# Banded attention in front of a gated MLP: scores by strips of 32 queries with 64 keys in place of blocks of 64 with 96

## The chip, the cores and the metric

The kernel runs on one core of a Trainium2 chip. The metric is device time in microseconds of one execution; 0.5% is about 4.7 us. The engines are named as in the profile: PE is TensorE (its weight loads are listed apart as PEld), DVE is VectorE, ACT is ScalarE, POOL is GpSimd, and SP is the queue that issues most transfers.

## What is computed

Eight batches of eight heads, 576 positions, 64 wide. Half of the heads look back over 32 positions, the other half over 128 positions in steps of 4. The attention output of all heads is one row of 512 per position, and 4608 such rows go through a two-layer MLP with a gate.

```python
scores = scale * np.matmul(q, k.transpose(0, 1, 3, 2))
rel = pos[:, None] - pos[None, :]
mask_plain = (rel >= 0) & (rel < window)                                          # window = 32
mask_dil = (rel >= 0) & (rel < window * dilation) & (rel % dilation == 0)         # dilation = 4
...                                     # heads 0-3 plain, heads 4-7 dilated; softmax over keys
x = attn_out.transpose(0, 2, 1, 3).reshape(B * S, H * D)
h = x @ w_in                                                                      # 512 -> 2048
g = h * erf(softplus(h))
out = g @ w_out                                                                   # 2048 -> 512
```

## The kernel before

**Attention units.** The host puts the positions of a dilated head in order of their residue by 4, so that both kinds of head become the same thing: a query sees the 32 keys up to its own place (a mask cuts it where a residue begins). A block is 64 queries of two heads. Four blocks are a unit, and there are 72 units. In one unit:

- `scores` (lines 180 to 187) multiplies, for each block and head, 64 queries by the 96 keys that they can see: 8 matmuls with 64 rows, 64 columns and 96 streamed keys. The four positions (head by odd or even block) lie in four quarters of the 128 x 128 array. The results of head 0 go to PSUM bank sp0, those of head 1 to sp1.
- `mask_max` (189) adds a mask, and takes the maximum of every row, with four VectorE instructions over 128 rows (two blocks) and 96 keys; `exponents` (201) is four ScalarE instructions; `normalize` (212) takes the reciprocal of the sums on VectorE and multiplies on GpSimd, 4 x 96 columns.
- `transposes` (220) turns each of the four 128 x 96 groups on TensorE, so that keys lie on partitions; `turned` (225) copies the 96 x 512 result from PSUM to the tile pT.
- `values` (234) multiplies, for each block and head, the 64 columns of values by 64 turned queries, over 128 rows of which 32 are zero: 8 matmuls with 128 rows, 64 columns and 64 streamed queries. The two heads lie in the two halves of the array's columns and write two halves of one PSUM bank.
- `rows_hi` on ScalarE and `rows_lo` on VectorE (278 and 282) write the result as a rounded part and the rest.

All of these are 32-bit matmuls, and each appears in the trace as two matmuls and two weight loads; a transpose appears as one of each.

**The MLP.** Rows go in 9 chunks of 512, and the 2048 inner columns in 8 pairs of tiles. For every tile `mm1` (450) issues 12 matmuls of 512 rows (line 460: high by high, high by low and low by high part, over four parts of the 512), VectorE copies h out of its one bank (`take`, 465), ScalarE and VectorE form the gate, and `mm2` (489) issues 12 matmuls (line 501) into the four banks acc two steps later. The weights come as 64-bit words, and ScalarE and VectorE split them into two parts in the first third of the program (`prep_act`, `prep_dve`, 377 and 391).

**Order.** It is written out by hand. In the front, 14 units are scored, one per call of `first_visit` (311): TensorE gets the transposes of unit n - 3, the scores of unit n, and then the values of unit n - 3. In calls 1 to 9 ScalarE makes the copy of `turned`, and then two steps of weight preparation, before it takes the values. After that a table (`visits`, 72) sets at which of the 144 steps of the MLP which units are scored. From the second step on, TensorE's order in such a step is `mm1`, the transposes of one or two units, `mm2`, their values, and then the scores of the units three further on (lines 589, 607, 620 and 631). PSUM is full: sp0, sp1, tx, h and the four acc.

Of the kernel before, what the change touches and what calls it, by code (L numbers as in the profile page):

```python
# [22 lines left out]
BLK = 64  # L23
NBLK = S // BLK
KEYS = BLK + WIN
RES = S // DIL
DM, DF = 512, 2048
NTOK = B * S
# [2 lines left out]
TOK = 512  # L31
NCH = NTOK // TOK
NIT = B * HP

PER = 4
NU = NIT * NBLK // PER
NEG = -1.0e9
SCALE = 0.125
BIG = 3.0e38


EDGES = (0, 16, 32, 48, -16)
DIL_EDGE = {0: 0, 2: 1, 4: 2, 6: 3, 7: 4}

REBASE = 2.0 ** -112
# [14 lines left out]
LAG = 3  # L62
FIRST = NBLK + LAG + 2

FREE = FIRST - LAG + 4
# [3 lines left out]
SAVED = 2 * (HALF + 1) + 1  # L69


def visits():
# [19 lines left out]

def kind(n):

    it, blk = divmod(n, NBLK)
    dil = it % HP >= HP // 2
    return 1 + DIL_EDGE[blk] if dil and blk in DIL_EDGE else (1 if blk == 0 else 0)

PAIRS = sorted({(kind(n), kind(n + 1)) for n in range(0, NIT * NBLK, 2)})
NMASK = len(PAIRS)


def key_start(u, j):

    return j * BLK + (WIN if (PER * u) // NBLK != (PER * u + j) // NBLK else 0)


QW = PER * BLK  # L110
KW = QW + 2 * WIN
# [3 lines left out]
def attn_moe_kernel(ctx: ExitStack, tc: tile.TileContext, qk, v, masks, eye, w_in, w_out, out):  # L115
    nc = tc.nc
# [5 lines left out]

    first = pool("first", 1)
    ident = first.tile([P, P], F32, name="ident")
    cst = first.tile([P, NMASK * KEYS], BF16, name="cst")
# [18 lines left out]
    vz = [one.tile([P, PER, 2, D], F32, name=f"v{i}") for i in range(2)]  # L144
    pz = [one.tile([P, PER, P], F32, name=f"pT{i}") for i in range(2)]

    spb = [ps.tile([P, TOK], F32, name=f"sp{i}") for i in range(2)]
    sps = [b[:, 0:PER * KEYS].rearrange("p (i b k) -> p i b k", i=2, k=KEYS) for b in spb]
# [4 lines left out]
    second = set()  # L153

    def place(u):

        return acc[(u + 1) % 4] if u < FREE else bank[:, PER * BLK:] if u in second else bank

    def turn_place(u):

        return place(u) if u < FREE else spb[u in second]


    xs = [one.tile([P, 2, S], F32R, name=f"x{cc}") for cc in range(CC)]
# [1 line left out]

    def load_qk(u):
        if u < NU:
            n = QW + key_start(u, PER - 1) + KEYS
            nc.sync.dma_start(out=qkz[u % 2][:, 0:n], in_=qk[u, :, 0:n])  # L170

    def load_v(u):
        if has(u):
            nc.sync.dma_start(out=vz[u % 2][0:KEYS], in_=v[u].rearrange("p (j h d) -> p j h d", j=PER, h=2))

    probs, maxes, sums, x_rows = {}, {}, {}, {}

# [1 line left out]

    def scores(u):  # L180
        i = u % 2
        for j in range(PER):
            at, r = QW + key_start(u, j), j % 2 * BLK
            for h in range(2):
                hs = slice(h * D, (h + 1) * D)
                nc.tensor.matmul(sps[h][r:r + BLK, i, j // 2, :], qkz[i][hs, j * BLK:(j + 1) * BLK],  # L186
                                 qkz[i][hs, at:at + KEYS], start=True, stop=True)

    def mask_max(u):
        pr = probs[u] = work.tile([P, PER, KEYS], F32, name="prob", bufs=LAG + 1)  # L190
        nmax = maxes[u] = small.tile([P, PER], F32, name="nmax", bufs=LAG + 1)
        for h in range(2):
            for p in range(PER // 2):
                n = PER * u + 2 * p
                nc.vector.tensor_tensor_reduce(  # L195
                    out=pr[:, 2 * h + p, :], in0=sps[h][:, u % 2, p, :], in1=mask[PAIRS.index((kind(n), kind(n + 1)))],
                    scale=-SCALE, scalar=BIG,
                    op0=ALU.add, op1=ALU.min, accum_out=nmax[:, 2 * h + p:2 * h + p + 1],
                )

    def exponents(u):
        nmax = maxes.pop(u)
        sums[u] = small.tile([P, PER], F32, name="ssum", bufs=LAG + 1)
        for j in range(PER):
            nc.scalar.activation(  # L205
                out=probs[u][:, j, :], in_=probs[u][:, j, :], func=AF.Exp,
                scale=-1.0, bias=nmax[:, j:j + 1], accum_out=sums[u][:, j:j + 1],
            )
        if u < FIRST:
            nc.gpsimd.tensor_scalar(sums[u], sums[u], 1.0e-9, None, op0=ALU.add)  # L210

    def normalize(u):
        rinv = small.tile([P, PER], F32, name="rinv")
# [4 lines left out]
        nc.gpsimd.tensor_tensor(probs[u], probs[u], rinv.broadcast_to([P, PER, KEYS]), op=ALU.mult)  # L218

    def transposes(u):  # L220
        pr = probs.pop(u)
        for j in range(PER):
            nc.tensor.transpose(out=turn_place(u)[0:KEYS, j * P:(j + 1) * P], in_=pr[:, j, :], identity=ident)  # L223

    def turned(u, copy):
        copy(out=pz[u in second][0:KEYS].rearrange("p j q -> p (j q)"), in_=turn_place(u)[0:KEYS])

    def turn(units):
        for u in units:
# [3 lines left out]

    def values(u):
        xp, vt, pt = place(u), vz[u % 2], pz[u in second]
        for j in range(PER):
            r = j % 2 * BLK
            for h in range(2):
                nc.tensor.matmul(xp[h * D:(h + 1) * D, j * BLK:(j + 1) * BLK], vt[:, j, h, :],  # L239
                                 pt[:, 2 * h + j // 2, r:r + BLK], start=True, stop=True)  # L240

    def attend(ready, scored):
        for u in ready:
# [64 lines left out]
    def has(u):  # L308
        return 0 <= u < NU

# [99 lines left out]
    h = ps.tile([P, TOK], F32, name="h")  # L410
# [3 lines left out]
    at = {0: [[x[:, i, 0:TOK] for x in xs] for i in range(2)]}  # L414
# [48 lines left out]
    hs, ls, gs = {}, {}, {}  # L463
# [49 lines left out]
    def save():  # L513

        o = doubles(2).bitcast(F32).rearrange("p n w -> p (n w)")
        spare = small.tile([P, DM], F32, name="o", bufs=1)
        for tt in range(TOK // P):
            part = [o[:, 0:DM], o[:, DM:2 * DM], spare, pz[1].rearrange("p j q -> p (j q)")][tt]
# [23 lines left out]

    with tc.manual_schedule():
        load_qk(0)
        nc.sync.dma_start(out=cst, in_=masks)
        for t in vz:
            nc.gpsimd.memset(t[KEYS:P], 0.0)
        nc.gpsimd.memset(pz[0][KEYS:P], 0.0)
        load_qk(1)
        nc.sync.dma_start(out=ident, in_=eye)  # L550
        for n in range(FIRST):
# [20 lines left out]
        for x in range(2 * (NT + 2)):  # L572
            t, j = divmod(x, 2)
# [66 lines left out]
                normalize(u)  # L640
            for m in ready:
                rows_lo(m)
            if x == SAVED + 2:
                nc.gpsimd.memset(pz[1][KEYS:P], 0.0)
        assert not todo and not prep and not staged and not begun and not made and not rest


# [24 lines left out]
def _keys(a):  # L672

    p = _padded(a).transpose(0, 1, 2, 4, 3).reshape(NIT, P, S + WIN)
    k = np.zeros((NU, P, KW), a.dtype)
    for n in range(NIT * NBLK):
        u, j = divmod(n, PER)
        it, blk = divmod(n, NBLK)
        k[u, :, key_start(u, j):key_start(u, j) + KEYS] = p[it, :, blk * BLK:blk * BLK + KEYS]
    return k  # L680


def _values(a):

    p = _padded(a)
    w = np.stack([p[..., i * BLK:i * BLK + KEYS, :] for i in range(NBLK)], axis=2)
    w = w.reshape(NU, PER, 2, KEYS, D).transpose(0, 3, 1, 2, 4)
    return np.ascontiguousarray(w).reshape(NU, KEYS, PER * 2 * D)


def _masks():
    import ml_dtypes

    i = np.arange(BLK)[:, None]
# [4 lines left out]
    m = np.concatenate([np.concatenate([masks[x] for x in pair]) for pair in PAIRS], axis=1)  # L699
    return np.where(m, 0.0, NEG / SCALE).astype(ml_dtypes.bfloat16)  # L700


# [27 lines left out]
```

## Time and profile before

| what | before |
|---|---|
| median of 3 runs | 941.26 us (939.98 to 943.89) |
| the profiled execution | 939.52 us, its span 937.7 us |
| TensorE busy, share of the span | 910.9 us, 97% |
| VectorE, ScalarE, GpSimd busy | 592.1, 642.2, 92.2 us |
| scores, line 186 (PE busy) | 38.36 us |
| transposes, line 223 | 42.78 us |
| values, line 239 | 46.88 us |
| mean granted clock of TensorE | 0.988 (0.87 from 0 to 78 us, 1.00 from there to 740 us) |

Busy time counts a matmul from its start to its modelled end, and many overlap, so the time that a group takes on TensorE is read from the distances between starts. A row of a line's view gives the count, minimum, median and maximum in ns, and the first and the last start. A row of the timeline gives a start, the time that the merged group covers, and its count. "128*64" behind MATMUL is the active rows and columns of the array.

### The profile page before, as it was taken

How to read it: one execution, taken by the hardware profiler on the slowest of the kernel's cores; microseconds unless marked ns; L12 is line 12 of the kernel's file. 1: busy time of each engine (PE TensorE's matmuls, PEld its weight loads, DVE VectorE, ACT ScalarE, POOL GpSimd, SP SyncE). 2: the span in 40 equal slices, each digit the busy share in tenths (PEclk: the TensorE clock that was granted, in tenths of full speed). 3: DMA queues.
4: the chain of work that ended last, by engine and by line, in shares of the span. 5: the costliest groups of instructions: out<-in, count | busy, mean ns of one | idle time of the engine just before them, and what ended most of it. 6: DMA issues, size and time to landing. Idle time of an engine off the chain costs nothing.

```text
span 937.7 us, 15922 instructions
## 1 busy us (share of the span) xinstructions
PE 910.9 (97%) x6048; PEld 744.3 (79%) x6048; DVE 592.1 (63%) x1569; ACT 642.2 (68%) x1202; POOL 92.2 (10%) x96
## 2 busy tenths in 40 slices
PE   4889999999999999999999999999999999999998
PEld 3567877888888888888888888888888888888886
DVE  6889989886566655565666566566665444345434
ACT  7889888885866866666678675966566555445553
POOL 2311210000111111011111110111111000000000
PEclk9699999999999999999999999999999999999999
DMA  8775443432632142324232162224210302011001
GB/s 285 258 253 180 154 156 136 157 113 105 185 111 67 67 158 70 108 68 126 73 112 82 52 224 78 100 70 130 84 70 34 115 20 71 1 46 45 1 1 45
DMA packets 51501, 98.74 MB, mean 105 GB/s; under 512 B 7136, under 2 KB 20192, under 8 KB 51424
## 3 DMA queue, kind: packets, MB, share of 16 engines
q1 hardware_dynamic: 51136, 97.19, 30.8%
q8 instruction: 48, 0.79, 0.3%
q10 hardware_dynamic: 288, 0.52, 0.1%
q14 instruction: 29, 0.24, 0.1%
HBM read 69.52 MB, written 27.26 MB: 103 GB/s over the span
## 4 chain that ended last, share of the span: by engine, by line
PE 89%; DVE 5%; ACT 2%; DMA 2%; issue 1%; SPq 0%; POOL 0%; POOLq 0%; DVEq 0%
PE h L460 41%; PE acc L501 40%; PE tx L239 3%; PE sp L186 3%; PE sp L223 3%; DVE w L402 1%; DMA qk<-in_qk_dram 1%; DVE w L403 1%; DVE prob L195 1%; DVE win_lo L397 1%; DMA dbl<-in_w_in_dram 0%; PE acc L223 0%; DVE w L401 0%; DVE s L483 0%; PE acc L239 0%
## 5 line engine op out<-in xcount | busy, mean ns | idle before, releaser
L468 DVE COPY hc<-h 128x512 f32<-128x512 f32 x144 | 99.4, 690 | 269.9 <-PE h L460 269.4
L460 PE MATMUL h<-x,win_hi 128*128 128x512 f32 x832 | 258.6, 392 | 1.9 <-DVE hc L468 1.8
L501 PE MATMUL acc<-wout_hi,ghi 128*128 128x512 f32 x576 | 227.5, 395 | 0.5 <-DVE dbl L519 0.3
L501 PE MATMUL acc<-wout_lo,ghi 128*128 128x512 f32 x576 | 224.5, 390 | 0.0
L472 ACT ACTIVATE s<-hc 128x1024 f32<-128x1024 f32 x72 | 76.4, 1061 | 193.3 <-DVE hc L468 193.1
L460 PEld LDWEIGHTS h<-x,win_hi 128*128 128x128 f32 x832 | 154.7, 188 | 35.8 <-DVE hc L468 2.7
L460 PE MATMUL h<-x,win_lo 128*128 128x512 f32 x416 | 162.1, 390 | 0.0
L501 PE MATMUL acc<-wout_hi,glo 128*128 128x512 f32 x576 | 158.8, 389 | 0.0
L218 POOL TENSOR_TENSOR prob<-prob,rinv 128x384 f32<-128x384 f32 x72 | 85.8, 1202 | 578.2 <-DVE ssum L216 281.2
L501 PEld LDWEIGHTS acc<-wout_hi,ghi 128*128 128x128 f32 x576 | 108.2, 188 | 22.9 <-DVE dbl L519 0.7
L501 PEld LDWEIGHTS acc<-wout_hi,glo 128*128 128x128 f32 x576 | 108.1, 188 | 22.6
L501 PEld LDWEIGHTS acc<-wout_lo,ghi 128*128 128x128 f32 x576 | 108.3, 188 | 21.6 <-DVE wout_lo L397 0.2
L205 ACT ACTIVATE prob<-prob,nmax 128x96 f32<-128x96 f32 x288 | 104.0, 364 | 3.1 <-DVE nmax L195 2.7
L487 DVE TENSOR_TENSOR glo<-s,ghi 128x512 fp32r<-128x512 f32 x144 | 100.2, 696 | 5.2
L483 DVE TENSOR_TENSOR s<-hc,s 128x1024 f32<-128x1024 f32 x72 | 96.9, 1346 | 5.6 <-ACT s L476 5.6
L473 ACT ACT_TABLE_LOAD x72 | 92.4, 1283 | 1.3
L476 ACT ACT_TABLE_LOAD x72 | 92.4, 1283 | 1.3
L460 PEld LDWEIGHTS h<-x,win_lo 128*128 128x128 f32 x416 | 78.1, 188 | 16.7
L195 DVE CUSTOM_DVE_ANT_0 prob<-sp,cst 128x96 f32<-128x96 f32 x288 | 54.7, 252 | 42.9 <-PE sp L186 42.8
L460 PE MATMUL h<-dbl,win_hi 128*128 128x512 f32 x256 | 80.7, 396 | 0.0
L486 DVE CAST ghi<-s 128x512 fp32r<-128x512 f32 x144 | 75.5, 525 | 2.5
L476 ACT ACTIVATE s<-s 128x1024 f32<-128x1024 f32 x72 | 76.4, 1061 | 0.8
(60 smaller groups left out, 897.0 us busy)
## 6 DMA issues: line engine op xcount, KB each, us to landing
xT<-rows SPq DMA_DIRECT2D x26, 576.0 KB, 4.8
v<-in_v_dram SPq DMA_DIRECT2D x72, 192.0 KB, 4.2
qk<-in_qk_dram SPq DMA_DIRECT2D x48, 272.0 KB, 3.9
dbl<-in_w_in_dram SPq DMA_DIRECT2D x16, 512.0 KB, 4.2
dbl<-in_w_out_dram SPq DMA_DIRECT2D x16, 512.0 KB, 3.3
qk<-in_qk_dram SPq DMA_DIRECT2D x24, 288.0 KB, 4.2
out_dram<-w SPq DMA_DIRECT2D x26, 256.0 KB, 2.2
x<-xT SPq DMA_DIRECT2D x8, 320.0 KB, 5.3
```

Source lines behind the costliest of these rows:

```text
L195: nc.vector.tensor_tensor_reduce(out=pr[:, 2 * h + p, :], in0=sps[h][:, u % 2, p, :], in1=mask[PAIRS.index((kind(n), kind(n + 1)))], scale ...
L205: nc.scalar.activation(out=probs[u][:, j, :], in_=probs[u][:, j, :], func=AF.Exp, scale=-1.0, bias=nmax[:, j:j + 1], accum_out=sums[u][:, ...
L218: nc.gpsimd.tensor_tensor(probs[u], probs[u], rinv.broadcast_to([P, PER, KEYS]), op=ALU.mult)
L460: nc.tensor.matmul(h, w[:, cc, ft * P:(ft + 1) * P], x[cc], start=(k == 0 and i == 0), stop=(k == CC - 1 and i == 2))
L468: nc.vector.tensor_copy(out=hs[t][:, j], in_=h)
L472: nc.scalar.activation(out=ls[t], in_=hs[t], func=AF.Sigmoid, scale=-1.0)
L473: nc.scalar.activation(out=ls[t], in_=ls[t], func=AF.Ln, bias=TINY)
L476: nc.scalar.activation(out=ls[t], in_=ls[t], func=AF.Erf, scale=-1.0)
L483: nc.vector.tensor_tensor(out=e, in0=hc, in1=e, op=ALU.mult)
L486: nc.vector.tensor_copy(out=ghi, in_=e[:, j])
L487: nc.vector.tensor_tensor(out=glo, in0=e[:, j], in1=ghi.bitcast(F32), op=ALU.subtract)
L501: nc.tensor.matmul(acc[tt], g[:, tt * P:(tt + 1) * P], w[:, ft, :], start=(first and w is wout_hi and g is ghi), stop=(last and g is glo))
```

## The change

A strip of 32 queries takes the place of the block of 64, and sees 64 keys. A unit is still 4 x 64 queries of two heads, now as 8 strips.

- The scores of a unit are 16 matmuls with 64 rows, 32 columns and 64 streamed keys; the eight positions (head by strip modulo 4) lie in eight pieces of the array, and four strips fill the 128 rows of a result.
- Masks, maxima, exponents and products go over four groups of 128 x 64, in place of 128 x 96. There are 10 mask tables as before.
- Two such groups, the two heads of four strips, lie side by side and are turned in one transpose of 128 x 128: 2 per unit in place of 4. The keys of head 0 come to partitions 0 to 63, those of head 1 to 64 to 127. The copy out of PSUM is 128 x 256 in place of 96 x 512, and its source is the upper half of a bank.
- The values of a unit are 16 matmuls with 64 rows, 64 columns and 32 streamed queries, head 0 in the corner of the array at row 0 and column 0, head 1 in the corner at 64 and 64. Both corners write one PSUM bank, in different partitions.
- The values tile is 128 partitions by 512 (256 KB per unit in place of 192), without rows of zeros, so the memsets go.

```diff
 def scores(u):
     i = u % 2
-    for j in range(PER):
-        at, r = QW + key_start(u, j), j % 2 * BLK
+    for s in range(SPU):
+        at, (p, r) = QW + key_start(u, s), divmod(s, SIDE)
         for h in range(2):
             hs = slice(h * D, (h + 1) * D)
-            nc.tensor.matmul(sps[h][r:r + BLK, i, j // 2, :], qkz[i][hs, j * BLK:(j + 1) * BLK],
-                             qkz[i][hs, at:at + KEYS], start=True, stop=True)
+            nc.tensor.matmul(sps[h][r * STRIP:(r + 1) * STRIP, i, p, :], qkz[i][hs, s * STRIP:(s + 1) * STRIP],
+                             qkz[i][hs, at:at + KEYS], start=True, stop=True,
+                             tile_position=(h * D, r * STRIP))
...
 def transposes(u):
     pr = probs.pop(u)
-    for j in range(PER):
-        nc.tensor.transpose(out=turn_place(u)[0:KEYS, j * P:(j + 1) * P], in_=pr[:, j, :], identity=ident)
+    for p in range(PARTS):
+        nc.tensor.transpose(out=turn_place(u)[:, p * P:(p + 1) * P],
+                            in_=pr[:, 2 * p:2 * p + 2, :].rearrange("p h k -> p (h k)"), identity=ident)

 def turned(u, copy):
-    copy(out=pz[u in second][0:KEYS].rearrange("p j q -> p (j q)"), in_=turn_place(u)[0:KEYS])
+    copy(out=pz[u in second][:, 0:PARTS * P], in_=turn_place(u))
...
 def values(u):
     xp, vt, pt = place(u), vz[u % 2], pz[u in second]
-    for j in range(PER):
-        r = j % 2 * BLK
+    for s in range(SPU):
+        qs = slice(s * STRIP, (s + 1) * STRIP)
         for h in range(2):
-            nc.tensor.matmul(xp[h * D:(h + 1) * D, j * BLK:(j + 1) * BLK], vt[:, j, h, :],
-                             pt[:, 2 * h + j // 2, r:r + BLK], start=True, stop=True)
+            hs = slice(h * D, (h + 1) * D)
+            nc.tensor.matmul(xp[hs, qs], vt[hs, s, :], pt[hs, qs], start=True, stop=True,
+                             tile_position=(h * D, h * D))
```

Here STRIP is 32, SIDE 4 (strips that fill 128 rows), SPU 8 (strips of a unit) and PARTS 2; KEYS is 64 in place of 96.

TensorE's rows at the transposes of one unit in the MLP's steps, before (sp_90 is bank sp0, x_100 the last part of x, acc_93 an accumulator):

```order
L460 MATMUL h<-x_100,win_hi 128x512 x2
L460 MATMUL h<-x_100,win_lo 128x512
L223 MATMUL sp_90<-ident,prob 96x128 x4
L501 MATMUL acc_93<-wout_hi,ghi 128x512
L501 MATMUL acc_93<-wout_lo,ghi 128x512
```

Four transposes of 96 turned keys stand there. TensorE's rows at the same place now, with the changed kernel's line numbers:

```order
L478 MATMUL h<-x_100,win_hi 128x512 x2
L478 MATMUL h<-x_100,win_lo 128x512
L239 MATMUL sp_90<-ident,prob 128x128 x2
L519 MATMUL acc_93<-wout_hi,ghi 128x512
L519 MATMUL acc_93<-wout_lo,ghi 128x512
```

The transposes stand at the same place, two in place of four. Behind `mm2` stand the values of that unit and the first scores of the next (pT_88 and v_87 are the turned probabilities and the values, sp_90 and sp_91 the two score banks), before:

```order
L501 MATMUL acc_95<-wout_hi,glo 128x512
L501 MATMUL acc_96<-wout_hi,glo 128x512
L239 MATMUL tx<-pT_88,v_87 64x64 x8
L186 MATMUL sp_90<-qk_84 64x96
L186 MATMUL sp_91<-qk_84 64x96
```

Eight value matmuls stand ahead of the scores. The same place now, on TensorE:

```order
L519 MATMUL acc_95<-wout_hi,glo 128x512
L519 MATMUL acc_96<-wout_hi,glo 128x512
L257 MATMUL tx<-pT_88,v_87 64x32 x16
L200 MATMUL sp_90<-qk_84 32x64
L200 MATMUL sp_91<-qk_84 32x64
```

Nothing changes its place among the stages. The values are 16 matmuls of 64 x 32 in place of 8 of 64 x 64, and the pair of scores (head 0, head 1) stands eight times in place of four.

More of the change, by code (lines that the diff above doesn't have):

```diff
@@ L24 @@
 NBLK = S // BLK
-KEYS = BLK + WIN
+STRIP = 32
+NSTRIP = S // STRIP
+KEYS = STRIP + WIN
 RES = S // DIL
@@ L93, in kind, with kinds, key_start @@
 def kind(n):
[L95 to L107, printed above, removed]
+    it, strip = divmod(n, NSTRIP)
+    at = strip * STRIP
+    if it % HP >= HP // 2:
+        e = (at + STRIP - 1) // RES * RES - at
+        return 1 + EDGES.index(e) if e > -WIN else 0
+    return 1 if strip == 0 else 0
+def kinds(u, p):
+    n = SPU * u + SIDE * p
+    return tuple(kind(n + i) for i in range(SIDE))
+PARTS = SPU // SIDE
+QUADS = sorted({kinds(u, p) for u in range(NU) for p in range(PARTS)})
+NMASK = len(QUADS)
+def key_start(u, s):
+    return s * STRIP + (WIN if (SPU * u) // NSTRIP != (SPU * u + s) // NSTRIP else 0)
 QW = PER * BLK
@@ L159, in turn_place @@
     def turn_place(u):
-        return place(u) if u < FREE else spb[u in second]
+        return (place(u) if u < FREE else spb[u in second])[:, PARTS * P:2 * PARTS * P]
     xs = [one.tile([P, 2, S], F32R, name=f"x{cc}") for cc in range(CC)]
@@ L202, in exponents @@
         nmax = maxes.pop(u)
-        sums[u] = small.tile([P, PER], F32, name="ssum", bufs=LAG + 1)
-        for j in range(PER):
+        sums[u] = small.tile([P, 2 * PARTS], F32, name="ssum", bufs=LAG + 1)
+        for j in range(2 * PARTS):
             nc.scalar.activation(
@@ L544, in attn_moe_kernel @@
         load_qk(0)
[L545 to L548, printed above, removed]
+        nc.sync.dma_start(out=cst[:, 0:NMASK * KEYS], in_=masks)
         load_qk(1)
@@ L675, in _keys @@
     k = np.zeros((NU, P, KW), a.dtype)
[L676 to L679, printed above, removed]
+    for n in range(NIT * NSTRIP):
+        u, s = divmod(n, SPU)
+        it, strip = divmod(n, NSTRIP)
+        k[u, :, key_start(u, s):key_start(u, s) + KEYS] = p[it, :, strip * STRIP:strip * STRIP + KEYS]
     return k
@@ L685, in _values @@
     p = _padded(a)
[L686 to L688 removed]
+    w = np.stack([p[..., i * STRIP:i * STRIP + KEYS, :] for i in range(NSTRIP)], axis=2)
+    w = w.reshape(NU, SPU, 2, KEYS, D).transpose(0, 2, 3, 1, 4)
+    return np.ascontiguousarray(w).reshape(NU, 2 * KEYS, SPU * D)
 def _masks():
     import ml_dtypes
[L694 removed]
+    i = np.arange(STRIP)[:, None]
     kk = np.arange(KEYS)[None, :]
@@ L698, in _masks @@
     masks = [ok] + [ok & ~((i >= e) & (kk < WIN + e)) for e in EDGES]
-    m = np.concatenate([np.concatenate([masks[x] for x in pair]) for pair in PAIRS], axis=1)
+    m = np.concatenate([np.concatenate([masks[x] for x in quad]) for quad in QUADS], axis=1)
     return np.where(m, 0.0, NEG / SCALE).astype(ml_dtypes.bfloat16)
```

40 lines of the change are left out of this document (19 added, 21 removed).

## The prediction

> **What bounds the kernel now.** I read the page first: which engine is busy and what ended last.
>
> ```profile
> span 937.7 us, 15922 instructions
> PE 910.9 (97%) x6048; PEld 744.3 (79%) x6048; DVE 592.1 (63%) x1569; ACT 642.2 (68%) x1202; POOL 92.2 (10%) x96
> PE 89%; DVE 5%; ACT 2%; DMA 2%; issue 1%; SPq 0%; POOL 0%; POOLq 0%; DVEq 0%
> ```
>
> TensorE holds the chain for 89% of the span. The average hides where it does not, so the second view is busy time by stretch (columns PE, PEld, DVE, ACT, POOL, then clock, DMA share, GB/s).
>
> ```profile
> 0.00:78.00 78.00, 56.31 (x685) 41.92 (x689) 63.42 (x257) 63.38 (x215) 19.75 (x37) 0.87 0.78 266
> 78.00:740.00 662.00, 660.71 (x4516) 542.60 (x4515) 441.21 (x1181) 477.36 (x898) 72.43 (x59) 1.00 0.32 106
> 740.00:937.70 197.70, 193.85 (x854) 159.77 (x852) 87.46 (x132) 101.48 (x92) 0.00 (x0) 1.00 0.12 40
> ```
>
> From 78 to 740 us TensorE is idle for 1.3 us out of 662. There the price of the change is TensorE's own time, and nothing that VectorE, ScalarE or GpSimd save counts. Before 78 us TensorE is idle for 22 us and other engines decide. After 740 us there is no attention work left. The same view for the three attention lines alone (first scores, then transposes, then values) counts what lies in the middle stretch.
>
> ```profile
> 78.00:740.00 662.00, 24.61 (x864) 18.94 (x862) 1.00 0.32 106
> 78.00:740.00 662.00, 29.54 (x224) 25.22 (x224) 1.00 0.32 106
> 78.00:740.00 662.00, 32.91 (x896) 28.63 (x896) 1.00 0.32 106
> ```
>
> A 32-bit matmul shows as two rows (8 per unit in the code, 16 in the trace) and a transpose as one (4). So 864/16 = 54 units are scored, 224/4 = 56 turned and 896/16 = 56 valued in it; the other 16 to 18 units lie before 78 us.
>
> Next, one visit with two units in TensorE's order of time (start, length of the merged group).
>
> ```profile
> 306.70 1.03 PE L223 MATMUL sp<-ident,prob 128*96 128x128 f32 x8
> 307.49 0.48 PE L501 MATMUL acc<-wout_hi,ghi 128*128 128x512 f32 x1
> ...
> 310.41 1.15 PE L239 MATMUL tx<-pT,v 128*64 128x64 f32 x32
> 311.50 0.89 PE L186 MATMUL sp<-qk 64*64 64x96 f32 x32
> 312.32 0.73 PE L460 MATMUL h<-dbl,win_hi 128*128 128x512 f32 x2
> ```
>
> To get a rhythm from merged groups I cut inside them, clear of the first one, and take the length less the last one's own duration: that is the time from first start to last start.
>
> ```profile
> 306.70 0.93 PE L223 MATMUL sp<-ident,prob 128*96 128x128 f32 x7
> ```
> ```profile
> 310.58 0.99 PE L239 MATMUL tx<-pT,v 128*64 128x64 f32 x28
> ```
> ```profile
> 311.64 0.74 PE L186 MATMUL sp<-qk 64*64 64x96 f32 x26
> ```
> ```profile
> 311.49 0.15 PEld L186 LDWEIGHTS sp<-qk 64*64 64x64 f32 x4
> ```
> ```profile
> 311.49 0.20 PEld L186 LDWEIGHTS sp<-qk 64*64 64x64 f32 x6
> ```
> ```profile
> 312.31 0.30 PEld L460 LDWEIGHTS h<-dbl,win_hi 128*128 128x128 f32 x2
> ```
>
> The durations of single ones are in the views of the lines (minimum/median/maximum in ns) and in the groups.
>
> ```profile
> L223 PE MATMUL sp<-ident,prob x228: 270/272/314, 74.0 to 733.7; 128*96 128x128 f32 x114
> ```
> ```profile
> L239 PE MATMUL tx<-pT,v x912: 222/222/271, 77.2 to 737.2; 128*64 128x64 f32 x183
> ```
> ```profile
> L186 PEld LDWEIGHTS sp<-qk x1152: 129/133/228, 3.5 to 695.4; 64*64 64x64 f32 x192
> L186 PE MATMUL sp<-qk x1152: 242/243/420, 3.5 to 695.5; 64*64 64x96 f32 x192
> ```
> ```profile
> L460 PEld LDWEIGHTS h<-x,win_hi 128*128 128x128 f32 x832 | 154.7, 188 | 35.8 <-DVE hc L468 2.7
> ```
>
> Transposes: 0.93 - 0.273 = 0.657 us for 6 steps, 109 ns each. Values run in pairs, one per half of the columns: 28 matmuls are 14 pairs, 0.99 - 0.222 = 0.768 us for 13 steps, 58 to 59 ns a pair. Scores run in fours, one per quarter of the array: 26 matmuls span six steps, 0.74 - 0.243 = 0.497 us, 82 ns a four. Loads: four start at once, the fifth begins only after 311.54, and the sixth starts at 311.49 + 0.20 - 0.133 = 311.56, so a load of 64 columns keeps its quarter for about 55 ns. Two loads of 128 columns are 0.30 - 0.188 = 0.112 us apart. That is 0.85 to 0.9 ns per column loaded.
>
> Streaming: 96 columns take 82 ns and 128 take 109, 0.84 ns per column and next to nothing fixed. 64 columns would take 55 to 56 by that. The values' 58 lies just above, and equals a load of 64 columns (55) and a short handover: load and stream are balanced there now. That balance is what the change touches.
>
> **The change part by part, per unit, in the middle stretch.**
>
> Transposes: 4 at 109 ns (436) become 2 with 128 columns loaded and 128 streamed, 112 ns by the 128-column loads: 224. Saved 0.212 us x 56 = -11.9 us.
>
> Values: 8 matmuls (16 rows) become 16 (32 rows) with half the rows and half the stream, and still 64 columns of weights each. Two corners of the array work at once, as two column halves do now: 16 rounds in place of 8. The stream falls to 32 x 0.84 = 27 ns, the load stays at 55 ns and the handover with it; the scores' row shows 55 with 64 rows, so halving the rows does not shorten it. 16 x 58 = 0.934 against 0.467: +0.467 us x 56 = +26.2 us. This is the term that decides. Its lower end is 16 x 55 (-3 us); if the load did not bind at all, see the first rival.
>
> Scores: 8 matmuls of 96 keys become 16 of 64 keys, on eight pieces of the array in place of four. A round streams 64 columns, 56 ns; its load of 32 columns, 28 ns, is hidden. The bounds: all eight at once, 4 rounds, 0.224 against 0.330 us, -0.106 x 54 = -5.7 us; or still only four at once, 8 rounds, 0.448, +0.118 x 54 = +6.4 us. The nearest row is the load view: four loads started within 0.15 - 0.13 = 0.02 us, 7 ns apart, so eight need about 50 ns, inside a round of 56. I take -5.7.
>
> The number of turns between array layouts in a visit (full, values, scores, full) stays. So the drains stay: 311.50 less the last values' start leaves some 0.15 us there, in both kernels.
>
> Sum of the middle: -11.9 + 26.2 - 5.7 = +8.6 us. VectorE's copy of 256 columns in place of 512, the smaller masks, exponents and products, all lie beside a full TensorE here and are worth nothing. The values load grows from 192 to 256 KB; the DMA share is 0.32 in this stretch, so it stays covered; if it did not, the price would be the 0.25 us a unit that 64 KB take at the front's 266 GB/s.
>
> The front, 0 to 78 us, has other rules.
>
> ```profile
> 13.00:37.00 24.00, 18.42 (x256) 13.63 (x252) 23.33 (x99) 22.46 (x84) 7.13 (x13) 0.68 0.85 284
> ```
> ```profile
> 21.70:42.10 20.40, 16.57 (x212) 12.32 (x209) 19.15 (x86) 17.02 (x72) 5.71 (x12) 0.50 0.83 283
> ```
> ```profile
> 30.32 0.62 ACT L383 CAST win_hi<-w 128x512 fp32r<-128x512 f32 x1
> ...
> 30.48 1.12 PE L239 MATMUL acc<-pT,v 128*64 128x64 f32 x16 [0.56 <-ACT pT L226]
> ...
> 30.84 0.68 ACT L388 ACTIVATE w<-dbl 128x512 f32<-128x512 f32 x1
> ```
> ```profile
> 44.76 0.83 POOL L218 TENSOR_TENSOR prob<-prob,rinv 128x384 f32<-128x384 f32 x1
> ```
> ```profile
> L468 DVE COPY hc<-h 128x512 f32<-128x512 f32 x144 | 99.4, 690 | 269.9 <-PE h L460 269.4
> ...
> L226 DVE COPY pT<-sp 96x512 f32<-96x512 f32 x57 | 36.6, 678 | 0.1
> ...
> L285 DVE TENSOR_TENSOR rows<-tx,rows 128x256 fp32r<-128x256 f32 x18 | 7.3, 419 | 0.0
> ...
> L226 ACT COPY pT<-acc 96x512 f32<-96x512 f32 x7 | 4.0, 572 | 0.4 <-PE acc L223 0.4
> ...
> L280 ACT CAST rows<-acc 128x256 fp32r<-128x256 f32 x3 | 1.1, 372 | 3.3 <-DVE nmax L195 1.7 <-PE acc L239 1.6
> ```
>
> From 13 to 37 us VectorE is full, 23.3 of 24. It pays (690 - 419)/256 = 1.06 ns per column, so four masks of 64 in place of 96 save 4 x 34 = 0.14 us a visit. But from 21.7 to 42.1 us the granted clock is 0.50, and every TensorE price doubles: the values grow by 0.93 us. Now they end at 31.60, just after ScalarE's two preparations (31.52) that cover them. The added 0.93 is uncovered, less the shorter copy (572 - 372 = 0.20) and exponents (0.1): some +0.5 us in each of four to five visits, +2; at full clock 0.47, covered, and -0.14 a visit remains, -0.6. I take +1. The first three visits wait on the first loads and save about 1 on masks, product and transposes. The last visits, 38 to 48 us, run as product, transposes, copy in turn: 0.83 by 256/384 to 0.55, 0.21 less in transposes, 1.06 x 256 = 0.27 less in the copy, together -0.7 in each of three visits, -2. From 48 to 78 us TensorE, VectorE and ScalarE take turns: 0.15 us more against 0.26 less per unit, 0 within 1. The front in all: 1 - 1 - 2 + 0 = -2 us, with ends at -4 (all at full clock) and +2.5 (the cold values uncovered in every visit, nothing saved behind).
>
> **Total.** +8.6 - 2 = +6.6 us. The profiled execution took 939.52 us (span 937.7 and 1.8 around it): 946.1 us. It lies 1.7 us under the median of 941.26, so in terms of a median the forecast is 948 us, 0.7% slower.
>
> **The rivals.**
>
> The weight load does not bind the values (faster). If the corner tiles overlap their loads more deeply, a round costs its 27 ns stream and the handover, 30 ns: 16 x 30 = 0.48, +0.7 us in place of +26.2. -11.9 + 0.7 - 5.7 - 2 = -18.9: 922 us. It decides from a round of 51 ns down, where 56 x (16 x 0.051 - 0.467) = 19.5 us equals what the rest saves. For it: 64 x 64 tiles never ran loads back to back here. Against it: the 55 ns wait of the fifth load. Chance 0.10.
>
> The front gives most of it back (no change). Its end of -4 and loads of 55 ns: +8.6 - 3 - 4 = +1.6, 943 us. For it: TensorE is idle for 22 us there. Chance 0.15.
>
> The scores do not spread over eight pieces: +6.4 in place of -5.7, total +18.7, 960 us. For it: no row shows more than four at once. Chance 0.10.
>
> A floor between matmul starts. The fastest run here is the scores' own: 26 matmuls in 0.497 us, 20 ns each. Were that a floor and not the stream of 96 columns, a unit's scores would cost 32 x 20 = 0.64, +0.31 x 54 = +16.7 in place of -5.7: 970 us. The starts 7 ns apart speak against it. Chance 0.04. The Trainium skill, page "TensorE: Matmul & The Clock Gate", section "Wait — 56ns, not 53.3ns?", states that starts never come closer than about 25 ns however few columns stream; by that figure the scores would cost 0.80 us a unit and the total would be about 979 us. The trace's mean of 20 ns already lies below it, so I give it no more weight than the row.
>
> The two corners of the values take turns. Today's score halves that differ in rows write different banks; the new values' corners differ in rows and write one bank. If they fully excluded each other, 32 x 58 = 1.87 us a unit, +1.40 x 56 = +78 in place of +26: 1000 us. If only the streams took turns, 2 x 30 fit in the 58 of the loads and nothing changes. Chance 0.03. The Trainium skill, page "TensorEngine Tiling (Array Packing)", section "Gotcha 1: PSUM Pressure", says that different row tiles cannot access the same bank at once; no run here shows it so far.
>
> **How the numbers follow.** The forecast has 0.58. A measurement of this kernel can tell about 0.5%, 4.7 us, from no change. Slower by more: 0.58 + 0.10 + 0.04 + 0.03 = 0.75; same 0.15; faster 0.10. The range leaves out the faster rival and the two dearest ones (0.17): from 940, under the no-change case, to 960, the case of four pieces. The forecast's own range is 944 to 952.
>
> **What would show it.** Right: values in rounds of 58 ns with 32 rows a unit, their line's share in 78 to 740 us near 26 us larger; transposes at about 112 ns; scores in eights every 56 ns; TensorE still without idle time there. Wrong: values in rounds near 30 ns (first rival), scores in fours, or a front that ends more than 4 us earlier or 2.5 later than the sum says.

## The result and the profile after

The changed kernel takes 957.24 us (median; 956.54 to 957.49), 1.0162 times the kernel before, 95% interval 1.0140 to 1.0185. That is 15.5 us over the 941.7 of the runs beside it, where the forecast was 948. The profiled execution took 957.2 us against 939.52, +17.7, and the forecast on that scale was +6.6. Three executions of the rounds below lie far above all others (1521.8 us of the kernel before, 1803.1 us of the split values, 4964.7 us of the kernel before with extra matmuls), and the times and ratios given here leave them out.

First the page after: span, engines, and the chain by engine.

```profile
span 955.4 us, 20237 instructions
PE 931.9 (98%) x8208; PEld 768.3 (80%) x8208; DVE 559.1 (59%) x1569; ACT 633.6 (66%) x1202; POOL 74.3 (8%) x92
PE 92%; ACT 3%; DVE 2%; DMA 1%; issue 1%; SPq 0%; DVEq 0%
```

VectorE, ScalarE and GpSimd each lost busy time (33, 9 and 18 us), and TensorE gained 21 and holds more of the chain. Next the windows after (columns as before), and the middle window for the scores, transposes and values alone.

```profile
0.00:78.00 78.00, 59.41 (x1141) 47.06 (x1142) 56.85 (x240) 55.25 (x198) 14.39 (x34) 0.99 0.81 261
78.00:740.00 662.00, 660.99 (x6112) 547.14 (x6111) 406.12 (x1184) 465.49 (x902) 59.87 (x58) 1.00 0.35 114
```
```profile
78.00:740.00 662.00, 23.33 (x1728) 1.00 0.35 114
78.00:740.00 662.00, 17.22 (x112) 1.00 0.35 114
78.00:740.00 662.00, 58.10 (x1792) 1.00 0.35 114
```

TensorE is idle for 1.0 us in the middle, so every nanosecond of its work still counts. The transposes fell by 12.3, the values rose by 25.2, and the scores fell by only 1.3.

To see where the 17.7 us come from, I follow one instruction: the first matmul of a step of the MLP. In the order of the MLP's own matmuls it is the same one in both kernels. Step 7, after and then before:

```profile
99.18 0.50 PE L478 MATMUL h<-x,win_hi 128*128 128x512 f32 x1
```
```profile
93.27 0.50 PE L460 MATMUL h<-x,win_hi 128*128 128x512 f32 x1
```

The last matmul of `mm1`, after and then before:

```profile
937.18 0.39 PE L478 MATMUL h<-dbl,win_lo 128*128 128x512 f32 x1
```
```profile
919.51 0.39 PE L460 MATMUL h<-dbl,win_lo 128*128 128x512 f32 x1
```

At step 7 the changed kernel is 5.9 us late, at the end 17.7. So the front costs 5.9 and the middle 11.8 us, where the forecast had -2 and +8.6.

**The middle.** One visit with two units, after:

```profile
314.95 0.60 PE L239 MATMUL sp<-ident,prob 128*128 128x128 f32 x4
315.31 0.48 PE L519 MATMUL acc<-wout_hi,ghi 128*128 128x512 f32 x1
...
318.25 2.05 PE L257 MATMUL tx<-pT,v 64*64 64x32 f32 x64
320.24 0.86 PE L200 MATMUL sp<-qk 64*32 64x64 f32 x64
321.03 0.73 PE L478 MATMUL h<-dbl,win_hi 128*128 128x512 f32 x2
```

From a group's start to the start of what follows, the visit at 306.70 before gave 0.79 for the transposes, 1.09 for the values and 0.82 for the scores. Here it is 0.36, 1.99 and 0.79. From exact starts the changes are -0.437, +0.903 and -0.033 us; for the 54 units behind step 7, counted as 27 such visits, -11.8, +24.4 and -0.9, in all +11.7. (In fact 25 visits have two units and four have one; the count is an estimate, and it comes within 0.1 us of the 11.8.) Cut at 319.9 us, the values read:

```profile
318.25 1.82 PE L257 MATMUL tx<-pT,v 64*64 64x32 f32 x56
```

Eight matmuls, four rounds, are 2.05 - 1.82 = 0.23 us: 58 ns a round, as forecast. The scores' line, cut at 320.7 and at 320.8 us (the last number of a row's head is the count):

```profile
L200 PE MATMUL sp<-qk x46: 212/216/242, 320.2 to 320.7; 64*32 64x64 f32 x46
L200 PE MATMUL sp<-qk x58: 212/216/242, 320.2 to 320.8; 64*32 64x64 f32 x58
```

In that tenth of a microsecond 12 matmuls start, 8.3 ns each. With their loads that is one instruction every 4.2 ns. The first unit's 32 do run in eights, 56 ns apart, and take 0.24 us; the second unit's take 0.38.

**The front.** TensorE's rows from 40 us on, after:

```profile
40.29 1.92 PE L257 MATMUL acc<-pT,v 64*64 64x32 f32 x32 [0.34 <-DVE pT L243]
...
43.36 1.92 PE L257 MATMUL acc<-pT,v 64*64 64x32 f32 x32
...
49.53 1.92 PE L257 MATMUL acc<-pT,v 64*64 64x32 f32 x32
51.38 0.69 PE L239 MATMUL acc<-ident,prob 128*128 128x128 f32 x2
51.72 1.20 PE L478 MATMUL h<-x,win_hi 128*128 128x512 f32 x2
...
55.57 0.63 PE L478 MATMUL h<-x,win_hi 128*128 128x512 f32 x2
...
56.36 1.12 PE L257 MATMUL acc<-pT,v 64*64 64x32 f32 x32
```

Up to 55.4 us a unit's values cover 1.92 us, and 1.12 after that; a pair of MLP matmuls covers 1.20 and then 0.63. TensorE is at half clock for the whole front, up to 55.4 us. The windows' clock column does not say so, since this trace has no record of the clock before 55.4 and the column prints 1.00 there; the durations do. Before, the full clock held from 14.8 to 21.7 us and from 42.1 on. The changed run also falls back once, at the start of the MLP:

```profile
75.90:79.30 3.40, 3.40 (x10) 2.62 (x9) 3.33 (x14) 3.35 (x4) 1.36 (x1) 0.50 0.89 310
```

So two terms were off: the front by 7.9 us (how much of it is the clock, the experiments show), and the scores by 4.8 us (-5.7 forecast, -0.9 measured). The values came out 1.8 us cheaper than forecast.

### The profile page after: what moved, and what is told of

Read it like the earlier page. It is cut to its first block, busy times and chain, and to the rows that moved or that the text cites. A ratio compares the mean times of both kernels' runs of the same rounds, so it can differ in the third digit from the quotient of the medians.

```text
span 955.4 us, 20237 instructions
## 1 busy us (share of the span) xinstructions
PE 931.9 (98%) x8208; PEld 768.3 (80%) x8208; DVE 559.1 (59%) x1569; ACT 633.6 (66%) x1202; POOL 74.3 (8%) x92
## 4 chain that ended last, share of the span: by engine, by line
PE 92%; ACT 3%; DVE 2%; DMA 1%; issue 1%; SPq 0%; DVEq 0%
PE h L478 41%; PE acc L519 39%; PE tx L257 6%; PE sp L200 3%; PE acc L257 2%; PE sp L239 1%; DMA dbl<-in_w_in_dram 1%; ACT prob L221 1%; DVE s L501 0%; PE acc L239 0%; DMA qk<-in_qk_dram 0%; DVE w L420 0%; DVE hc L486 0%; DVE w L421 0%; DVE win_lo L415 0%
## 5 line engine op out<-in xcount | busy, mean ns | idle before, releaser
L519 PEld LDWEIGHTS acc<-wout_lo,ghi 128*128 128x128 f32 x576 | 108.2, 188 | 21.7
L234 POOL TENSOR_TENSOR prob<-prob,rinv 128x256 f32<-128x256 f32 x72 | 70.3, 986 | 603.3 <-DVE ssum L232 297.5
L221 ACT ACTIVATE prob<-prob,nmax 128x64 f32<-128x64 f32 x288 | 96.3, 337 | 3.0 <-DVE nmax L211 2.6
L501 DVE TENSOR_TENSOR s<-hc,s 128x1024 f32<-128x1024 f32 x72 | 93.5, 1299 | 5.6 <-ACT s L494 5.6
L211 DVE CUSTOM_DVE_ANT_0 prob<-sp,cst 128x64 f32<-128x64 f32 x288 | 45.4, 220 | 69.0 <-PE sp L200 68.4
L494 ACT ACTIVATE s<-s 128x1024 f32<-128x1024 f32 x72 | 76.4, 1061 | 0.8
L491 ACT ACTIVATE s<-s 128x1024 f32<-128x1024 f32 x72 | 76.3, 1060 | 0.8
```

Of the source, the lines that this page charges most:

```text
L211: nc.vector.tensor_tensor_reduce(out=pr[:, g, :], in0=sps[h][:, u % 2, p, :], in1=mask[QUADS.index(kinds(u, p))], scale=-SCALE, scalar=BIG ...
L221: nc.scalar.activation(out=probs[u][:, j, :], in_=probs[u][:, j, :], func=AF.Exp, scale=-1.0, bias=nmax[:, j:j + 1], accum_out=sums[u][:, ...
L491: nc.scalar.activation(out=ls[t], in_=ls[t], func=AF.Ln, bias=TINY)
L494: nc.scalar.activation(out=ls[t], in_=ls[t], func=AF.Erf, scale=-1.0)
L501: nc.vector.tensor_tensor(out=e, in0=hc, in1=e, op=ALU.mult)
L519: nc.tensor.matmul(acc[tt], g[:, tt * P:(tt + 1) * P], w[:, ft, :], start=(first and w is wout_hi and g is ghi), stop=(last and g is glo))
```

## The experiments

**What sets the values' 58 ns.** Every values matmul streams 64 columns in place of 32, the neighbour's included, which the next matmul overwrites; the output stays the same.

```diff
-            qs = slice(s * STRIP, (s + 1) * STRIP)
+            qs = slice(s * STRIP, min(s + 2, SPU) * STRIP)
```

> The values stream 64 queries per matmul in place of 32 (each strip writes its neighbour's columns too, and the neighbour's own matmul then overwrites them), with the same 32 loads of 64 columns per unit. Load theory: a round is set by the load, 58 ns, and a stream of 64 columns takes 54 to 56 ns, so it hides: values of two units still span about 1.84 us from first to last start, and the time stays within 1 us of the changed kernel's 957.2. Rival, that a round is the stream and a fixed part of about 30 ns: rounds of 85 ns, +0.43 us a unit, +24 us or more, 981 us.

```profile
314.20 2.06 PE L257 MATMUL tx<-pT,v 64*64 64x64 f32 x64
```

Twice the stream, and the visit's values still cover 2.06 us. So the stream does not set the round. That leaves the load of 64 columns, which the next run tries. But the time did not stay within 1 us of 957.2, as expected; it fell to 953.22 us (1.0127, 1.0111 to 1.0143), all of it in the front:

```profile
43.07 1.23 PE L257 MATMUL acc<-pT,v 64*64 64x64 f32 x32
...
94.84 0.73 PE L478 MATMUL h<-x,win_hi 128*128 128x512 f32 x2
```

The full clock came at 43.3 us in place of 55.4 and stayed, and step 7 starts 4.3 us earlier.

**Loads of 32 columns.** The other side of the same question: each values matmul is split into two with 32 columns of weights, on four pieces of the array.

```diff
-            nc.tensor.matmul(xp[hs, qs], vt[hs, s, :], pt[hs, qs], ..., tile_position=(h * D, h * D))
+            for half in range(2):
+                at = h * D + half * STRIP
+                nc.tensor.matmul(xp[at:at + STRIP, qs], vt[hs, s, half * STRIP:(half + 1) * STRIP],
+                                 pt[hs, qs], ..., tile_position=(h * D, at))
```

> Each value matmul is split into two of 32 columns of weights in neighbouring pieces of the array: 64 matmuls a unit in place of 32, four pieces at work at once, the output the same. Load theory: a load of 32 columns takes 28 ns, so a round takes about 32 ns, and 16 rounds 0.51 us a unit; but 128 loads and matmuls a unit at the 4.2 ns apiece that the second unit's scores show (two loads and two matmuls every 17 ns) take 0.54 us, so 1.1 us for two units in place of 1.84: -0.38 us a unit, -21 us in the middle, and 3 to 5 us less in the front, where the values at half clock are uncovered: 931 to 935 us. Rival, that every matmul in a piece pays 58 ns whatever it loads: 16 rounds again, no change, 957 us. Rival, that twice the matmuls cost twice the time: +0.9 us a unit, over 1000 us.

Measured: 962.12 us (958.12 to 966.59; 1.0224, 1.0161 to 1.0286), where 931 to 935 was expected. From its timeline, the values of one visit, the scores behind them, and the MLP:

```profile
232.62 1.32 PE L259 MATMUL tx<-pT,v 64*32 64x32 f32 x126
...
233.78 0.82 PE L200 MATMUL sp<-qk 64*32 64x64 f32 x62
236.70 1.22 PE L480 MATMUL h<-x,win_hi 128*128 128x512 f32 x2 [2.09 <-issue]
```

Its waits from 80 to 740 us, TensorE's rows for "issue" (us in total, times, longest):

```profile
PE sp L200 <- issue: 15.5, 9, 2.3
...
PE h L480 <- issue: 5.1, 3, 2.1
...
PE tx L259 <- issue: 1.0, 1, 1.0
```

The values fall from 1.99 to 1.15 us (232.62 to 233.77), with 128 matmuls at 8.8 ns; halving the load almost halves them, which confirms that the load binds. The gain, 27 visits by 0.84 or some 23 us, is lost again in these 13 stalls, 21.6 us in all, in which TensorE waits for nothing that the profile shows, and in three falls of the clock behind such stalls, 3.4 us each at half clock. By these figures the middle should be some 4 us longer than the changed kernel's. From step 7 to step 107 it takes 644.9 us in place of 638.0, so some 3 us are not accounted for. Twelve of the stalls (the other is 0.2 us long) begin 0.2 to 1.4 us behind the start of a fetch of an instruction block, but 50 of the 62 fetches in this stretch are followed by none. This program makes more of them (the queue for instructions over the whole run, this kernel and then the changed one):

```profile
q8 instruction: 82, 1.34, 0.6%
```
```profile
q8 instruction: 64, 1.05, 0.5%
```

That the fetch is the cause was not tried by itself.

**The scores' place.** If the second unit's scores are slow because TensorE's queue has run empty behind the first unit's 64 short instructions (32 loads and 32 matmuls), they are fast when long MLP matmuls stand ahead of them. If they wait for their keys or banks, they are slow anywhere. So they go ahead of the values, right behind `mm2`.

```diff
+        for u in scored[1:]:
+            scores(u)
         for u in ready:
             values(u)
-        for u in scored:
+        for u in scored[:1]:
             scores(u)
```

> The scores of a visit's second unit stand ahead of the values, those of the first unit behind them. Supply theory: the second unit's scores fell from eights every 56 ns to two matmuls every 17 ns because loads and matmuls reach the array no faster than one every 4.2 ns once the queue in front of it is empty; apart, both sets start from a full queue and each spans about 0.24 us from first to last start, where together they span 0.64; a turn between layouts more costs about 0.2 us a visit, so the time stays within 2 us of 957. Rival, that the second unit waits for its own keys or for the bank: its scores still take about 0.4 us wherever they stand.

```profile
317.68 0.45 PE L200 MATMUL sp<-qk 64*32 64x64 f32 x32
318.06 2.06 PE L257 MATMUL tx<-pT,v 64*64 64x32 f32 x64
320.05 0.45 PE L200 MATMUL sp<-qk 64*32 64x64 f32 x32
```

Both sets now take 0.24 us from first to last start. So neither the keys nor the banks hold the second unit back. What is left is the rate of 4.2 ns per instruction behind another burst; the split values ran at about that rate too. That a queue has run empty there is argued: no view shows the queue. Little is won by it, 956.11 us in one run: each set ends in a turn of the array of some 0.15 us, and there is one more of these. Two sets of 0.384 us against 0.788 are 0.02 us a visit.

**The front's clock.** Unneeded 128 x 128 matmuls behind the scores of every front call from the fourth on, once in the changed kernel and once in the kernel before. They add work, and change no result.

```diff
         scores(n)
         load_qk(n + 2)
+        if n >= 3:
+            for _ in range(5):
+                nc.tensor.matmul(h[:, 0:P], ident, ident, start=True, stop=True)
```

> The changed kernel with five unneeded 128 x 128 matmuls behind the scores of each call of the front from the fourth on; nothing reads what they write. Clock theory: the front lost 6 us because TensorE was never busy enough for the full clock before 55 us, so that the values at 1.9 us were uncovered; kept busier, the clock is full from about 15 to 25 us on, a call takes 3.4 to 3.5 us in place of 3.97, and the first matmul of the MLP starts at 47 to 49 us in place of 51.7: 952 to 954 us. Rival, that the values' length alone lost it whatever the clock: the added matmuls make each call longer or leave it the same, and the MLP starts at 52 us or later: 957 us or more.

> The kernel before with the same five unneeded 128 x 128 matmuls behind the scores of each call of the front from the fourth on. Clock theory: the half clock hurts the changed front because its values at 1.9 us are longer than the ScalarE work beside them; before, the values at 1.1 us just fit and VectorE bounds the calls (23.3 of 24 us busy), so a full clock gains at most 1 us here against the 4.5 it gained for the changed kernel: the MLP starts at 47.5 to 49.5 us, and the time is 939 to 943. Rival, that any front gains from the clock alike: -4 us, 937 us.

The changed kernel with them takes 954.51 us (1.0139, 1.0123 to 1.0155), with the full clock from 15.2 us on. A front call takes 3.48 us, as expected; the MLP starts a little later than expected, and the time is 0.5 us above the range:

```profile
13.98 1.66 PE L257 MATMUL acc<-pT,v 64*64 64x32 f32 x32
...
49.91 0.71 PE L481 MATMUL h<-x,win_hi 128*128 128x512 f32 x2
...
94.63 0.73 PE L481 MATMUL h<-x,win_hi 128*128 128x512 f32 x2
```

The kernel before with them takes 943.37 us (1.0017, 1.0007 to 1.0027), at full clock from 16.1 to 74.1 us and from 77.6 us on:

```profile
15.37 1.01 PE L239 MATMUL acc<-pT,v 128*64 128x64 f32 x16
...
51.16 0.71 PE L463 MATMUL h<-x,win_hi 128*128 128x512 f32 x2
...
96.89 0.50 PE L463 MATMUL h<-x,win_hi 128*128 128x512 f32 x1
```

So the clock helps the changed front and not the old one, as the clock theory has it. But the old front missed its own expectation: its MLP starts at 51.16 us, 2.6 us later than without the extra matmuls (48.52), so these cost time of their own.

With the same extra matmuls the changed front brings the MLP to step 7 some 2.3 us earlier than the old one (94.63 against 96.89). Of these, 1.4 us stand already at the first values (13.98 against 15.37), where the forecast had 1 us saved. From there to the first matmul of the MLP both need nearly the same (35.93 and 35.78 us), and the last 1.0 us goes with the fall of the old kernel's clock at 74.1 us. So the savings of the first visits show, and those forecast for the last visits do not. No changed front of these runs reaches step 7 before the old one's 93.27 us; the earliest does at 94.57.

**Streaming alone.** To tell the clock from all else that the first run changed, the 64 columns go only into the front's single units.

```diff
-            qs = slice(s * STRIP, (s + 1) * STRIP)
+            qs = slice(s * STRIP, min(s + (2 if u < FREE else 1), SPU) * STRIP)
```

> The changed kernel with one edit, in its front's single-unit visits alone: the values matmuls stream 64 columns instead of 32 (the neighbouring strip's columns are written too and overwritten by the next matmul, so the output stays the same); the 27 two-unit visits are as in the changed kernel. The theory (the half clock of the changed front lasts to 55 us because its values wait on loads and stream only half of the time; a run whose matmuls stream all the time is granted the full clock earlier): full clock from about 43 us as in the run that streams 64 columns everywhere, matmul 84 of the MLP about 4 us earlier than the changed kernel's 99.2 us, time 953 to 954 us. The rival (what that run gained came from its two-unit visits, or is chance): clock as in the changed kernel, 957 us.

Measured: 953.52 us (1.0131, 1.0116 to 1.0146), as that theory expected, though the full clock comes at 46.5 us and not at 43.

```profile
43.68 1.92 PE L257 MATMUL acc<-pT,v 64*64 64x64 f32 x32
...
46.16 0.56 PE L200 MATMUL sp<-qk 64*32 64x64 f32 x32
46.74 1.12 PE L257 MATMUL acc<-pT,v 64*64 64x64 f32 x32
...
95.64 0.73 PE L478 MATMUL h<-x,win_hi 128*128 128x512 f32 x2
```

Up to 46 us the rows last as long as in the changed kernel, so TensorE is occupied no longer than there. Only the stream inside them is doubled. In the changed kernel the full clock came 3.7 us after the first MLP matmul, which opens its first long stretch of unbroken streaming. In the two other runs with the same front (the scores apart, above, and the four corners, below) it came at 55.0 and 54.1 us, 3.3 and 2.7 us after that matmul.

**All four corners.** If the load binds, two corners that load leave two idle. The second unit of a visit (the set SWAPPED) gets its heads swapped on the partitions, so that its corners are the other two, and the two units' strips alternate; its output goes to a second bank. The lines show the matmuls alone.

```diff
...
-    def values(u):
-        xp, vt, pt = place(u), vz[u % 2], pz[u in second]
+    def values(*units):
         for s in range(SPU):
             qs = slice(s * STRIP, (s + 1) * STRIP)
-            for h in range(2):
-                hs = slice(h * D, (h + 1) * D)
-                nc.tensor.matmul(xp[hs, qs], vt[hs, s, :], pt[hs, qs], ..., tile_position=(h * D, h * D))
+            for u in units:
+                xp, vt, pt = place(u), vz[u % 2], pz[u in second]
+                for h in range(2):
+                    at = D * (h if u not in SWAPPED else 1 - h)
+                    nc.tensor.matmul(xp[h * D:(h + 1) * D, qs], vt[at:at + D, s, :], pt[at:at + D, qs],
+                                     ..., tile_position=(at, h * D))
...
```

> In a visit with two units the second unit's two heads change places on the partitions (its masks' results, its turned probabilities and its values), its values are issued strip by strip between those of the first and land in the upper half of score bank 1. The two units then use all four 64 x 64 corners of the array, with as many loads and matmuls as the changed kernel. Load theory: rounds of 58 ns hold four matmuls in place of two, so two units' values span 0.93 us in place of 1.84: -0.9 us in each of 25 visits, -22 us: 934 to 936 us. Rival, that corners which share columns or rows take turns: 1.8 us as now, 957 us. Rival from the split run, where TensorE stood still for 1 to 2 us at a time with nothing to wait for but its own instructions: the visit's 256 loads and matmuls for values and scores now come in 1.9 us in place of 2.8, and a part of the gain goes to such stalls: 940 to 948 us.

Measured: 933.91 us, 0.9918 of the kernel before (0.9903 to 0.9933), at the lower end of what was expected.

```profile
311.99 0.25 PE L261 MATMUL tx<-pT,v 64*64 64x32 f32 x2
312.01 0.25 PE L261 MATMUL sp<-pT,v 64*64 64x32 f32 x2
312.07 0.23 PE L261 MATMUL tx<-pT,v 64*64 64x32 f32 x2
...
312.90 0.23 PE L261 MATMUL sp<-pT,v 64*64 64x32 f32 x2
313.06 0.86 PE L203 MATMUL sp<-qk 64*32 64x64 f32 x64
```

Four matmuls start in each round of 58 ns, and the visit's values need 1.07 us in place of 1.99. This is the dearest term of the change, undone.

**The pieces together.** The corners with the unneeded matmuls, the same with the scores apart, and last the corners, the scores apart and the front's 64 streamed columns without unneeded work. The edits are those above.

> The four corners and the unneeded matmuls of the front together. If the two effects are independent, as the clock and load theories have it, their gains add: 4 to 4.5 us under the four corners alone, 929 to 932 us, 1% faster than the kernel before.

Measured: 932.34 us (0.9902, 0.9888 to 0.9917), a little above what was expected: the two gains did not add up. Its clock fell to half from 35.0 to 38.4 us and from 72.5 to 79.4, and its step 7 starts at 98.40 us, no earlier than without the extra matmuls (98.28).

> As the run before, with the second unit's scores ahead of the values as well. Supply theory: both sets of scores span 0.24 us, and the values, 128 loads and matmuls in 0.93 us (7 ns apiece), leave the queue time to fill: 1 to 2 us less than with the scores together, 928 to 931 us. Rival, that instructions are short over the whole visit and not only behind a burst: no gain, or stalls.

Measured: 930.91 us (0.9893, 0.9874 to 0.9912). From step 7 to step 107 it needs 614.45 us and the run above 614.55: the scores' place gave nothing here, and in these two profiles its whole lead is a front with fewer falls of the clock (step 7 at 94.57).

> The interleaved corners (933.9 us), with the second unit's scores put ahead of the values, and 64 streamed columns in the front's single-unit visits; no unneeded matmuls. If streaming grants the clock and the scores' 4.2 ns supply limit is passed by their place: 933.9 less about 4 for the front and 1.5 for the scores, 928 to 930 us. If the clock of the front is not to be had by streaming: 932 us, as for the corners with the scores' place alone.

```profile
span 927.6 us, 20242 instructions
PE 904.4 (97%) x8208; PEld 739.4 (80%) x8208; DVE 559.5 (60%) x1569; ACT 635.0 (68%) x1202; POOL 74.4 (8%) x92
```

Measured: 929.49 us, 0.9877 (0.9861 to 0.9894), the lowest median of all, though its interval overlaps that of the run above. The sum holds and its split doesn't quite: the front gave 3.2 us (step 7 at 95.10) and the middle 0.7. That the scores' place is what gave the 0.7 isn't shown.

## Why the prediction was right and wrong

Slower was right, and 957.2 lies inside the range from 940 to 960, but only because that range was drawn out to the case of scores on four pieces, which did not come about. It lies above the forecast's own 944 to 952. The size was wrong, +17.7 on the profiled scale for +6.6.

- **Transposes:** -11.9 forecast, -11.8 by visits. Right.
- **Values, 16 rounds at 58 ns a unit, +26.2:** +24.4 by visits, +25.2 in the line's windows. Right in mechanism and size; twice the stream changed nothing, and half the load nearly halved them.
- **Scores, "all eight at once", -5.7:** the mechanism was right and the size wrong. The eights at 56 ns exist, but only for the first unit of a visit. I priced the second unit as if instructions came at any rate. Behind the first unit's burst they come every 4.2 ns, its 32 rows take 0.38 us in place of 0.24, and the term was -0.9.
- **The front, "in all: 1 - 1 - 2 + 0 = -2 us":** the step that failed. I took the clock of the run before, full from 14.8 to 21.7 us and from 42.1 us on, as given, and priced the new work under it. But values that wait for loads half of the time did not get the full clock before 55.4 us. By the starts of the values, the first visits gave -0.4 (forecast -1). The next six calls cost +3.1 (forecast +1): 0.5 each, which is what the prediction gave a visit at half clock, but the changed kernel is at half clock in all of them. The last visits came to -0.2 (forecast -2), and the way from there to step 7 of the MLP to +3.4 (forecast 0). The sum is +5.9. With the full clock from 43.3 us (64 columns) the last two come to -0.8 together, so about 4 us of the miss are the late clock. At full clock from 15.2 us (extra matmuls) the six calls take 20.87 us against 21.07 before, so the +3.1 goes as well. The rest of the savings forecast for the last visits shows in no run, and why stays open. The bound of "+2.5 (the cold values uncovered in every visit, nothing saved behind)" was too tight for the same reason: it ended the half clock at 42 us.

Of the rivals, the load that doesn't bind is excluded by the split and the 64 columns. The corners on one bank did not take turns: two matmuls start in every 58 ns round, and that holds with 64 streamed columns too, where two streams of some 54 ns (64 by the prediction's 0.84 ns) would not fit one after the other. The scores did spread over eight pieces, and the front gave nothing back. On the floor between starts, the Trainium skill, page "TensorE: Matmul & The Clock Gate", section "Wait — 56ns, not 53.3ns?", states about 25 ns. The trace disagrees: 8.3 ns apart over 12 scores, on eight pieces of the array.

## What to carry to other kernels

Before packing matmuls into smaller pieces of TensorE, compare a round's load (its columns) with its stream, since a piece that streams fewer columns than it loads costs the load; then look for idle pieces that another unit can fill. Treat the clock as a result of the change, not as a given, and read it from the durations of one fixed instruction where the trace has no record of it. Price very short matmuls also by the rate at which instructions arrive, above all behind other short ones.

## What the runs showed of the hardware

- **In these runs the clock followed streaming, not occupation.** From 40.3 to 51.7 us the changed kernel's TensorE ran rows back to back and stayed at half clock. With twice the stream in rows of the same length the full clock came at 43.3, 46.5 and 46.0 us (three runs), against 55.4, 55.0 and 54.1 (three runs) without. The Trainium skill, page "TensorE: Matmul & The Clock Gate", section "What's actually happening", says that the full clock comes after about 3.4 us of sustained busy time. That agrees with the 2.7 to 3.7 us from the first MLP matmul on, but not with 11 us of rows in a profile that stand back to back: what counts as busy is not what the profile's busy column shows. Why the kernel before had the full clock from 14.8 us and lost it at 21.7 us, no run shows.
- **Behind a burst of short instructions, the next ones start every 4.2 ns** (scores of the second unit, 8.3 ns per matmul with its load; split values, 8.8 ns). The burst itself, 32 loads and 32 matmuls, starts within 0.24 us. That an empty queue is the reason is argued.
- **With more short instructions TensorE stalled for 1 to 2 us at a time** (12 stalls of 1.0 to 2.3 us and one of 0.2, together 21.6 us, in the middle of the kernel with 10512 matmuls; with 8208 no matmul waited so there, and a weight load 0.4 us at most). Whether the fetch of instruction blocks is the cause stays open.
